# Window attention inside a fused attention and feed-forward kernel: 64-key score blocks on four 64x64 array tiles, one denominator matmul per head, values kept twice

## The chip, the cores and the metric

The kernel runs on one core of one Trainium2 chip. The metric is the device time of one execution in microseconds. The kernel before takes 311.0 us (median of 3 runs, 309.78 to 311.76). A profiled execution gives a span, which is some 1.7 us shorter than the device time that goes with it.

Engines: PE multiplies matrices, PEld loads its weights, VectorE (DVE), ScalarE (ACT) and GpSimd (POOL) work on elements, and SP issues DMA transfers, in the traces in the order of its program (in the changed kernel's second step from the query load at 77.71 us to the second value copy at 93.01).

## The reference

```python
# q, k, v: (8 batches, 8 heads, 576 positions, 64); float32
scores = (q @ k.T) / sqrt(64)
scores = where(abs(pos_q - pos_k) <= 32, scores, -1e9)
attn = softmax(scores) @ v                       # per head
x = attn.transpose(0, 2, 1, 3).reshape(4608, 512)
out = gelu_tanh(x @ w_in) @ w_out                # 512 -> 2048 -> 512
```

A query sees only keys within 32 positions. So only a band of each 576x576 score matrix is computed, in blocks of keys with the queries that can see them.

## The kernel before

Everything is built around PE. A step handles one tile of 512 rows of the feed-forward part, and into its output matmuls (112 of 256 columns; the first step has 64 of 512) a plan inserts the attention of the next batch: `s` is a group of scores, `m` its mask multiply, `v` the weighing of values, `x` the normalised result. A group is a pair of heads; group -1 is the tail of the batch before.

The scores use 128-key blocks, one matmul per head and block, both heads side by side on the two 64-row halves of the array (the cuts of code are shortened, `...` stands for what is left out):

```python
MAIN = [[(0, 0, 0, 40), (128, 1, 24, 72)], [(256, 2, 56, 104), (384, 3, 88, 120)]]
...
PLAN = {6: "s0 v-1", 24: "s1", 26: "m0", 31: "x-1", 40: "m1", 42: "v0 s2", 48: "x0", 56: "m2",
        61: "v1 s3", 64: "x1", 80: "m3", 81: "v2 s4", 88: "x2", 97: "v3", 104: "m4", 112: "x3"}
```

Neighbouring blocks overlap in queries (0 to 40 and 24 to 72, in units of four query rows). So the values and the row sums of a query are accumulated over two blocks, each with one pair of matmuls for the values `o` and one for the sums `d` (weights: a matrix of ones):

```python
for w, bk in ((0, o), (1, d)):
    for h in range(2):
        nc.tensor.matmul(bk[...], V[:, c, head, :] if w == 0 else ones, pes[hf][:, h, ...],
                         start=(i == 0), stop=(i == len(todo) - 1))
```

The fourth group is "fused" in the kernel before: values and ones of a head stand side by side as one 128-column weight, so that one matmul per head and block makes both `o` and `d`.

The first two batches get their values through float32 staging tiles and casts on GpSimd. From batch 2 on they are loaded and cast by DMA (`load_v`, issued by GpSimd), and queries and keys come by seven loads on SP (`load_qk`).

The softmax here doesn't subtract the row's maximum and nothing guards it: scores larger than these inputs give would overflow.

## Time and profile before

| what | before |
|---|---|
| time, median | 311.0 us |
| profiled span | 308.3 us |
| first output matmul of the first step | 39.04 us |
| first step (from there to the next first output matmul) | 34.26 us |
| second step | 32.22 us |
| third to seventh step | 31.60, 31.59, 31.75, 31.60, 31.59 us |
| granted PE clock, mean | 0.996 to 1.000 in ten runs |

The rows of steps are read from the timeline of PE, as the start of the first output matmul of each step. They cut the span into a prologue, two special steps and a steady part. The prediction below shows and reads the lines of the profile themselves.

### The profile page before, as it was taken

The numbers are of one execution on the slowest core, as the hardware profiler recorded it, in microseconds if no ns is written. First come the engines' busy times: TensorE is split into PE (matmuls) and PEld (weight loads), VectorE is DVE, ScalarE is ACT, GpSimd is POOL, SyncE is SP. The second block draws the span as 40 slices with busy tenths as digits, with TensorE's granted clock in tenths as the row PEclk, the third lists the DMA queues.
The fourth block names the chain that finished last, engine by engine and source line by source line (L and its number), as shares of the span: only waits on it lengthen the run. The fifth ranks groups of instructions, "written<-read, shape, count | busy, mean of one in ns | idle before, by whom it ended". The sixth has DMA issues, their size and how long they took to land.

```text
span 308.3 us, 6660 instructions
## 1 busy us (share of the span) xinstructions
PE 297.5 (97%) x2587; PEld 187.8 (61%) x2587; DVE 202.9 (66%) x462; ACT 202.4 (66%) x323; POOL 112.3 (36%) x174
## 2 busy tenths in 40 slices
PE   7889999999999999999999999999999999999993
PEld 2553545546784588458854885478647864784583
DVE  5663686886869676957785778766876655542451
ACT  1776477578677777778677868677767776606600
POOL 4558455069127421832084207620700070015000
PEclk9999999999999999999999999999999999999999
DMA  7999999999996999699969984999471031004013
GB/s 211 254 357 368 375 338 213 290 164 167 222 161 156 148 198 180 157 142 216 169 155 153 240 141 117 164 226 178 115 161 19 2 90 48 0 19 120 0 40 101
DMA packets 120254, 50.65 MB, mean 164 GB/s; under 512 B 101519, under 2 KB 113551, under 8 KB 120222
## 3 DMA queue, kind: packets, MB, share of 16 engines
q1 hardware_dynamic: 84329, 37.50, 54.9%
q0 software_dynamic: 34960, 11.54, 32.4%
q10 hardware_dynamic: 933, 1.18, 1.1%
q8 instruction: 20, 0.33, 0.5%
q14 instruction: 12, 0.10, 0.1%
HBM read 37.62 MB, written 9.44 MB: 153 GB/s over the span
## 4 chain that ended last, share of the span: by engine, by line
PE 84%; SPq 4%; DMA 3%; DVE 3%; ACT 2%; POOL 1%; issue 1%; POOLq 0%
PE mm L574 31%; PE mm L479 21%; PE ph L479 16%; PE ps_s L365 4%; PE mm L545 4%; DMA wst<-in_moe_w_in_dram 3%; PE ps_o L411 3%; PE ps_d L411 2%; SPq L136 1%; SPq L145 1%; POOL w_in L197 1%; PE ps_o L402 1%; SPq L188 1%; DVE t L509 1%; PE ps_d L402 1%
## 5 line engine op out<-in xcount | busy, mean ns | idle before, releaser
L479 PEld LDWEIGHTS <-w_in 128*128 128x128 f16 x576 | 56.0, 98 | 67.3 <-issue 1.8
L535 POOL DMA_DIRECT2D out_dram<-y x77 | 44.7, 588 | 114.1 <-DVE y L603 107.1
L479 PE MATMUL mm<-xT,w_in 128*128 128x512 f16 x320 | 78.0, 379 | 0.6 <-DVE xT L441 0.6
L487 ACT ACTIVATE gT<-mm 128x512 f16<-128x512 f32 x80 | 47.6, 599 | 36.2 <-PE mm L479 35.6
L479 PE MATMUL ph<-xT,w_in 128*128 128x512 f16 x256 | 64.4, 379 | 0.9 <-ACT gT L487 0.7
L574 PEld LDWEIGHTS <-s 128*128 128x128 f16 x512 | 48.9, 98 | 7.0
L519 DVE TENSOR_TENSOR s<-gT 128x512 f16<-128x512 f16 x64 | 26.8, 419 | 35.0 <-ACT gT L487 35.0
L371 ACT ACTIVATE pe<-ps_s 128x704 f16<-128x704 f32 x64 | 43.3, 728 | 9.0 <-PE ps_s L365 8.2
L574 PE MATMUL mm<-t,s 128*128 128x256 f16 x376 | 45.8, 273 | 0.0
L487 ACT ACTIVATE gT<-ph 128x512 f16<-128x512 f32 x64 | 36.3, 602 | 12.3 <-PE ph L479 12.1
L574 PEld LDWEIGHTS <-gT 128*128 128x128 f16 x384 | 36.0, 98 | 7.3
L176 POOL DMA_DIRECT2D V<-in_v_dram x30 | 28.5, 972 | 20.2 <-PE ps_d L411 14.3
L429 ACT ACTIVATE lt<-ps_d 128x480 f32<-128x480 f32 (+3 forms) x33 | 18.2, 553 | 22.6 <-PE ps_d L411 22.5
L574 PE MATMUL mm<-w_out,gT 128*128 128x256 f16 x256 | 32.8, 273 | 0.0
L380 DVE TENSOR_TENSOR pe<-pe,mask 128x704 f16<-128x704 f16 x64 | 30.7, 517 | 1.4 <-ACT pe L371 1.4
L441 DVE TENSOR_TENSOR xT<-ps_o,lt 128x480 f16<-128x480 f32 (+10 forms) x38 | 20.3, 547 | 16.1 <-ACT lt L430 16.0
L430 ACT ACTIVATE lt<-lt 128x480 f32<-128x480 f32 (+3 forms) x40 | 23.5, 587 | 1.3
L91 ACT ACT_TABLE_LOAD x17 | 21.8, 1283 | 1.1 <-PEq L814 0.8
L411 PEld LDWEIGHTS <-V 128*64 128x64 f16 x280 | 15.0, 109 | 9.0 <-issue 3.9
L365 PE MATMUL ps_s<-QT,KT 64*128 64x192 f16 (+5 forms) x336 | 17.9, 227 | 0.9 <-DVE KT L301 0.9
L411 PE MATMUL ps_d<-pe,ones 128*64 128x160 f16 (+2 forms) x208 | 17.6, 234 | 0.0
L411 PE MATMUL ps_o<-pe,V 128*64 128x192 f16 (+3 forms) x188 | 16.8, 241 | 0.7 <-DVE xT L441 0.4
(89 smaller groups left out, 325.5 us busy)
## 6 DMA issues: line engine op xcount, KB each, us to landing
kr<-in_k_dram SPq DMA_DIRECT2D x32, 256.0 KB, 7.9
qr<-in_q_dram SPq DMA_DIRECT2D x6, 1024.0 KB, 7.4
V<-in_v_dram POOLq DMA_DIRECT2D x30, 112.0 KB, 6.9
wst<-in_moe_w_in_dram SPq DMA_DIRECT2D x3, 1024.0 KB, 8.2
wst<-in_moe_w_out_dram SPq DMA_DIRECT2D x3, 1024.0 KB
qr<-in_q_dram SPq DMA_DIRECT2D x8, 256.0 KB
vr<-in_v_dram SPq DMA_DIRECT2D x16, 128.0 KB, 7.4
out_dram<-y POOLq DMA_DIRECT2D x24, 48.0 KB, 2.3
```

Source lines behind the costliest of these rows:

```text
L91: nc.scalar.add_instruction(mybir.InstLoadActFuncSet(name=nc.get_next_instruction_name(), act_func_set_id=which, ins=[], outs=[]))
L176: nc.gpsimd.dma_start(V[:, c, 0:7, :], v[b, 0:7, k0:k0 + 128, :].rearrange("h p d -> p h d"))
L365: nc.tensor.matmul(ps[:, h, off:off + 4 * n].rearrange("k (j p) -> k j p", j=4), KTs[b % 2][r0:r0 + 64, pr, k0:k0 + 128], QTs[b][r0:r0 + 6 ...
L371: nc.scalar.activation(pe, ps[:, :, 0:w], AF.Exp, scale=SCALE)
L380: nc.vector.tensor_tensor(pe, pe, m.rearrange("p (o w) -> p o w", o=1).broadcast_to(list(pe.shape)), op=ALU.mult)
L411: nc.tensor.matmul(bk[r0:r0 + 64, at:at + 4 * n].rearrange("d (j p) -> d j p", j=4)[:, :, p0 - q0:p1 - q0], V[:, c, 2 * pr + h + (pr == 3 ...
L430: nc.scalar.activation(lt[:, 0:n], lt[:, 0:n], AF.Exp, scale=-1.0)
L479: nc.tensor.matmul(ph, w_in16[:, dc, fc * 128:fc * 128 + 128], xT[:, dc, t * 512 % RING:t * 512 % RING + 512], start=(dc == 0), stop=(dc = ...
L487: nc.scalar.activation(gTs[t][:, fc, :], phs[fc], AF.Gelu_apprx_tanh)
L519: nc.vector.tensor_tensor(dst, x, y, op=op)
L535: (eng or turn_about[0] if t == NT - 1 else eng or nc.gpsimd).dma_start(out_v[b, j, q0 + p:q0 + p + e, cols], yo[m:m + e, cols])
L574: nc.tensor.matmul(pys["apart"][:, 0:256] if apart else py[:, blk, :], lhsT, wino[w][:, f, :], start=(new and i % (8 if one else 16) == 0) ...
```

## The change

Intent: fewer PE columns for the attention. Scores are made in 64-key blocks, so four 64x64 tiles of the array work at once (two heads times two key blocks). The queries are cut so that each query column is covered by one pair of 64-key blocks, and is written once. Then the row sums take one matmul per head. For the values, a query column needs 128 consecutive keys that start at a multiple of 64; so the values are kept twice, the second time shifted by 64 keys.

```diff
-MAIN = [[(0, 0, 0, 40), (128, 1, 24, 72)], [(256, 2, 56, 104), (384, 3, 88, 120)]]
+FIRST = [((0, 0, 24), (64, 0, 40)), ((128, 24, 56), (192, 40, 72)), ((256, 56, 88), (320, 72, 104))]
+MAIN = FIRST + [((384, 88, 120), (448, 104, 120))]
+SLOTS = [(0, 0, 24), (4, 24, 40), (1, 40, 56), (5, 56, 72), (2, 72, 88), (6, 88, 104), (3, 104, 120)]
...
-PLAN = {6: "s0 v-1", 24: "s1", 26: "m0", 31: "x-1", 40: "m1", 42: "v0 s2", 48: "x0", 56: "m2", ...
+PLAN = {5: "s0 v-1", 25: "m0 x-1", 27: "s1 v0", 40: "m1 x0", 49: "s2 v1", 62: "m2 x1", ...
...
+    def pair_v(b, copy, hs=slice(0, H)):
+        V = Vs[b % 2]
+        copy(V[64:128, 4:8, hs, :], V[64:128, 0:4, hs, :])
+        copy(V[0:64, 4:7, hs, :], V[0:64, 1:4, hs, :])
...
+    for i, q0 in ((2, 0), (3, 128), (0, 0), (1, 120)):      # masks: 21 small copies, the two halves in turn
+        for step in kinds[i]:
+            for half, piece in enumerate(step): ...
...
+        for h in range(2):                                  # row sums: one matmul per head
+            nc.tensor.matmul(d[64 * h:64 * h + 64, ...], ones, pe[:, h, :], start=True, stop=True)
...
         if t and b + 1 < B:
             load_qk(b + 1)
+        if t == 1:
+            pair_v(unpaired.pop(), nc.sync.dma_start)       # batch 2: two DMAs on SP
```

Batch 0 is paired by VectorE in the prologue, batch 1 by GpSimd in the first step, batch 2 and all later ones by two DMAs on SP, for batch 2 behind the seven loads that SP issues in the second step, and for later ones at the end of a step's program.

## The prediction

> **What bounds the kernel now.** I read the page first, then the chain of waits, then the timeline of each engine over one batch, with the start times of single matmuls.
>
> ```profile
> PE 297.5 (97%) x2587; PEld 187.8 (61%) x2587; DVE 202.9 (66%) x462; ACT 202.4 (66%) x323; POOL 112.3 (36%) x174
> PE   7889999999999999999999999999999999999993
> PE 84%; SPq 4%; DMA 3%; DVE 3%; ACT 2%; POOL 1%; issue 1%; POOLq 0%
> ```
>
> Engines, slices, chain: after the prologue TensorE (PE) has no gap, and it carries 84% of the chain. The rest of the chain is prologue (a 10.4 us wait for first-layer weights up to 25.8 us). So from 45 us on, a nanosecond of PE saved is a nanosecond of time, and any new PE wait is added in full.
>
> A batch step repeats every 31.6 us (124.12 to 155.71 in the chain). In it, 64 matmuls of 512 columns start 0.2155 us apart (13.8 us) and 112 of 256 columns 0.109 us apart (12.2 us). The other 5.55 us are attention: scores s, and weighing v (values "o" and row sums "d") for four head pairs and the tail.
>
> ```profile
> 142.08 1.25 PE L574 MATMUL mm<-w_out,gT 128*128 128x256 f16 x10
> 143.26 0.26 PE L411 MATMUL ps_o<-pe,V 128*64 128x160 f16 x2
> 143.35 0.24 PE L411 MATMUL ps_d<-pe,ones 128*64 128x160 f16 x2
> 143.42 0.25 PE L411 MATMUL ps_o<-pe,V 128*64 128x192 f16 x2
> 143.51 0.25 PE L411 MATMUL ps_d<-pe,ones 128*64 128x192 f16 x2
> ...
> 143.81 0.22 PE L411 MATMUL ps_d<-pe,ones 128*64 128x128 f16 x2
> 143.96 0.47 PE L365 MATMUL ps_s<-QT,KT 64*128 64x160 f16 x8
> 144.36 0.83 PE L574 MATMUL mm<-w_out,gT 128*128 128x256 f16 x6
> ```
>
> Columns: start, length, engine, line, operation, count. A pair of 192 columns (one head per array half) advances the start by 0.08 us, which is 192 columns at one per 0.42 ns: both heads stream together, 3 to 4 ns apart. At each change of array shape there is a hole: the last output matmul starts at 143.058, should free the array 0.109 later, and the weighing starts at 143.261: 94 ns lost. Likewise 98 ns into the scores, 96 out of them, plus 10 ns on the return to the full array and 23 behind the first short pair. Summed over a step with its 14 shape changes: scores 4 x 290 + 170, weighing 3 x 578 + 579 (the fused group) + 341, changes 1495, together 5.48 us, against 5.55 seen. So attention is column-bound plus shape changes, not bound by weight loads.
>
> [...] 3 to 4 ns between tiles, 94 to 98 ns a change. [...] In this trace, 64- and 32-column pairs of 128x64 weights (43.92 to 44.36 us) come every 32 ns whatever their width, where 64 columns would need 27; 96-column pairs take 42, as columns say. [...] issues go one after another and stretch to 4 us when the DMA engines are full. [...] Here the first eight 512-column matmuls take 3.59 us, 0.43 each, against 0.215 later.
>
> **The change, part by part, on PE (one batch step).**
> - Scores: per head 672 columns in two row tiles become 960 in four tiles, 480 columns of time. With full overlap 480 x 0.417 = 200 ns and some ns per step, 208 in place of 290: 4 x 82 = 0.33 us. The tail stays 170.
> - Denominators: one 480-column pair (205 ns). Values: one 96-column pair (42) and six 64-column pairs at the weight-load pace of 32 (192). Sum 439 in place of 578 (three groups) and 579 (fused): 3 x 139 + 140 = 0.56 us. The tail gains 0.01.
> - Shape changes: the fused group had none. Now five episodes go full, score, weigh, full at 96 + 94 + 107 = 297: 1485 in place of 1495. Nothing.
> - Sum: 0.9 us a step, 5.4 us over the six steps with the full plan. The first step (33 to 60 us) gains about 0.8 the same way and gives some back: its values are now paired by eight GpSimd copies (estimated 0.5 us each from the 0.61 us casts of 128x512) between a cast that ends at 46.2 and its use at 46.55. I count a net gain of 0.4.
> - ACT and DVE: one exponential of 960 columns for two (704 and 640; the second starts 638 ns after the first, the next 584 after that, so 853 by slope for 1222) and one mask multiply: slack, not time. Prologue: some 20 small mask copies and eight pairing copies more on DVE (about 1 us and 3.5 us), but weights arrive only at 25.8 while attention ends near 23.2: nothing.
>
> **First new wait.** The plan moves v0 from output matmul 42 to 27, and the tail's spread x-1 just ahead. Both use the one bank for "o".
>
> ```profile
> 137.93 1.28 ACT L91 ACT_TABLE_LOAD   x1
> 139.23 1.35 ACT L371 ACTIVATE pe<-ps_s 128x704 f16<-128x704 f32 x2
> 140.47 0.50 ACT L429 ACTIVATE lt<-ps_d 128x384 f32<-128x384 f32 x1
> 140.99 0.52 ACT L430 ACTIVATE lt<-lt 128x384 f32<-128x384 f32 x1
> ```
>
> Counted from the first output matmul (137.12): table load until 2.11, exponential 0.85, logarithm 0.53, inverse 0.52, spread 0.56: the bank is free at 4.6. PE gets to v0's "o" at 27 x 0.109 + 0.83 (s0, v-1) + 0.40 (s1 and changes) + 0.21 (d) = 4.4. A wait of about 0.25 us in each of five steps: 1.25 us back.
>
> **Second new wait, the large one.** Values stand twice, shifted by 64 keys; the second copy is made by two DMAs on SP, behind the load. In the built order of SP's instructions, batch 2's two copies stand after all seven loads of batch 3's queries and keys, and the second "o" weight load of batch 2 waits for both. In most steps SP is long done. In the step that starts at 73.3 us it is not:
>
> ```profile
> 74.69 0.40 SPq L166 DMA_DIRECT2D qr<-in_q_dram  x1
> 75.15 11.09 SPq L168 DMA_DIRECT2D kr<-in_k_dram  x4
> 86.29 2.75 SPq L170 DMA_DIRECT2D qt<-in_q_dram  x1
> 89.08 1.77 SPq L171 DMA_DIRECT2D kt<-in_k_dram  x1
> ```
>
> and from the DMA issues (last column: median us to landing):
>
> ```profile
> V<-in_v_dram POOLq DMA_DIRECT2D x30, 112.0 KB, 6.9
> kt<-in_k_dram SPq DMA_DIRECT2D x6, 128.0 KB, 4.2
> ```
>
> Two value loads and these loads share full engines there (DMA share over 1.5 in this stretch), so SP frees at 90.85. A tenth fewer value rows, and the 0.4 us gained, make that about 90. Two issues of 0.6 and 4.2 us to landing: about 94.5. PE wants the shifted values at 73.3 - 0.4 + 4.4 = 77.3. It stands for 17.2 us. Nothing hides it, since everything later is PE work. [...]
>
> Sum: 311.0 - 5.4 - 0.4 + 1.25 + 17.2 + 1.5 = 325.1.
>
> **Rivals.**
> 1. Pure PE gain, no new wait: 311.0 - 5.8 = 305.2. For it: PE is the bound and every saved column counts. Against it: SP's order, and a data dependence that no slack covers. It needs SP to issue its seven loads in a few us; the trace shows 16.
> 2. The copies land earlier, because SP's issues stretch less with less value traffic: at 86 the wait is 9 us and the total about 316. [...] Against: the q and k traffic, the larger part, is untouched.
> 3. The four score tiles don't overlap, or small weight loads bind: scores then take 400 ns or more, the 0.9 turns negative, and without the DMA wait the total would be 311 to 316. For: 64x64 weights appear nowhere in this trace. Against: pairs overlap in both directions. It only adds to my number: 330.
> 4. The extra copies overload the DMA engines in every step: 0.45 MB a batch in 3 and 4 KB runs against about 5 MB; in later steps SP is idle from 150.5 to 158.8, where they fit. Nothing.
>
> **Range and chances.** The order on SP and the dependence are facts of the program; only the landing time is estimated, from 88 to 97, which gives 318 to 328. To stay within 2% it must land before about 88 (a wait under 10); to be faster, SP would have to behave quite differently. Faster 0.06, within 2% 0.07, slower 0.87. Predicted 325.0 us, range 316 to 329.
>
> **What would show it.** Right: one hole in PE's slices near 77 to 95 us, ended by the DMA V<-V; steps of about 30.9 us elsewhere; score groups of some 0.21 us with four starts 4 ns apart; a spread ending PE waits of a quarter us in other steps. Wrong: no such hole, V<-V issued before 85, or steps that stay at 31.6 or grow.

The sum came to 325.1 us. Its last term, 1.5 us for a restart at half clock, is the author's estimate. The trace before gives about the same: eight 512-column matmuls, started 0.427 us apart in place of 0.2155, lose 1.7 us. The 1 and 3.5 us of VectorE's copies in the prologue are estimates too.

## The result, and the profile after

The changed kernel takes 330.06 us (median of 4 runs, 329.70 to 332.46), beside 311.02 us for the kernel before on the same chip (now 4 runs, 309.78 to 311.76). The ratio is 1.063 (95% interval 1.0585 to 1.0674), so it is slower. Ratios are the mean time of one kernel's fast runs over that of the other's of the same rounds, so not quite the ratio of the medians quoted. Executions over 1.5% slower than the fastest of the same kernel are left out of the means.

The page of the changed kernel, its first row, two of its rows of 40 slices, and the chain by engine:

```profile
PE 295.6 (90%) x2883; PEld 183.5 (56%) x2883; DVE 195.0 (59%) x436; ACT 185.9 (57%) x283; POOL 106.6 (32%) x167
PE   5968996999109999999999999999999999999994
PEclk9999999999858999999999999999999999999999
PE 82%; DVE 5%; SPq 5%; ACT 2%; issue 2%; DMA 2%; POOL 0%; POOLq 0%
```

PE has almost the same busy time as before (295.6 and 297.5 us) in a span 20 us longer, and the slices show where: a hole of about two slices (8.2 us each) near 82 to 98 us, and thinner work in the first, the third and the seventh slice (prologue and first step). The clock falls inside and behind the hole (0.50 from 88 to 101.7 us). VectorE's share of the chain has grown from 3 to 5%.

The steps, beside those before:

| part | before | after | difference | predicted difference |
|---|---|---|---|---|
| prologue, to first output matmul | 39.04 | 42.23 | +3.19 | 0 |
| first step | 34.26 | 36.06 | +1.80 | -0.4 |
| second step | 32.22 | 48.61 | +16.39 | +17.8 |
| third to seventh step together | 158.13 | 156.58 | -1.55 | -3.25 |
| rest of the span | 44.65 | 44.73 | +0.08 | 0 |
| sum | 308.30 | 328.21 | +19.91 | +14.15 |

The predicted column is the text's own terms, put where it puts them (the second step: -0.9 + 17.2 + 1.5).

**The large hole.** SP's timeline in the second step; columns are start, length, queue, line, operation:

```profile
77.71 0.40 SPq L163 DMA_DIRECT2D qr<-in_q_dram  x1
78.17 12.32 SPq L165 DMA_DIRECT2D kr<-in_k_dram  x4
...
92.43 0.53 SPq L180 DMA_DIRECT2D V<-V  x1
93.01 0.59 SPq L181 DMA_DIRECT2D V<-V  x1
```

and PE's timeline there, in brackets the time for which it stood still and what ended it:

```profile
84.14 0.23 PE L386 MATMUL ps_o<-pe,V 128*64 128x96 f16 x2 [0.17 <-DVE xT L415]
98.93 0.53 PE L386 MATMUL ps_o<-pe,V 128*64 128x64 f16 x12 [14.56 <-DMA V<-V]
```

The first pair of values needs only the unshifted slot 0 and goes at 84.14. The next needs the shifted slot 4. SP takes 12.3 us to issue four key loads, at a DMA share of 2.03 in that stretch (of the four, the first takes 0.58 us and the longest 5.70), reaches the two copies only at 92.43, and they land at 97.95 and 98.80. This is the wait that was foreseen.

**The prologue.** VectorE, before (its mask copies start at 1.96 us and the first query cast at 4.46), against VectorE in the changed kernel:

```profile
2.04 4.55 DVE L243 COPY mask<-full 64x96 f16<-64x96 f16 x21 [0.84 <-POOL full L232]
...
6.79 0.43 DVE L256 CAST q<-qr 128x512 f16<-128x512 f32 x1
```

The cast on which everything hangs is 2.33 us later. The 21 copies mostly start 0.20 us apart; the ten copies before started mostly 0.10 to 0.13 apart. PE stands 2.43 us for that cast, and runs at half clock for longer:

```profile
10.43 0.69 PE L357 MATMUL ps_s<-QT,KT 64*64 64x96 f16 x18
...
14.06 0.42 PE L357 MATMUL ps_s<-QT,KT 64*64 64x96 f16 x18 [0.17 <-DVE KT L293]
```

The same 18 matmuls take 0.69 us and then 0.42. The record of the clock has its first change, to full speed, at 12.98 us here and at 7.01 in the kernel before; PEclk and the mean clocks in this document count the time ahead of it as full speed, but matmuls of 512 columns there start 0.43 us apart, and 0.22 after it. Further on, PE in the changed kernel waits for pairing copies:

```profile
23.19 0.40 PE L386 MATMUL mm<-pe,V 128*64 128x64 f16 x14 [0.77 <-DVE V L181]
23.52 0.61 PE L447 MATMUL mm<-xT,w_in 128*128 128x512 f16 x2
...
25.64 0.40 PE L386 MATMUL ps_o<-pe,V 128*64 128x64 f16 x14 [1.14 <-DVE V L181]
```

Batch 0's attention ends at 26.0 us. Before, it ended at 21.2, and by the time the weights came (25.8) PE had already done 18 of the first-layer matmuls:

```profile
19.63 0.60 PE L479 MATMUL mm<-xT,w_in 128*128 128x512 f16 x2
...
21.79 0.59 PE L479 MATMUL mm<-xT,w_in 128*128 128x512 f16 x2 [0.58 <-DVE xT L441]
22.22 1.02 PE L479 MATMUL ph<-xT,w_in 128*128 128x512 f16 x4
23.08 0.59 PE L479 MATMUL mm<-xT,w_in 128*128 128x512 f16 x2
23.51 1.21 PE L479 MATMUL ph<-xT,w_in 128*128 128x512 f16 x4
24.89 1.04 PE L479 MATMUL ph<-xT,w_in 128*128 128x512 f16 x4 [0.17 <-POOL w_in L197]
```

Now it had done two.

**The first step.** VectorE's mask multiply takes 0.66 us when alone. The next one, during which GpSimd goes through copies and casts without a pause, takes 2.63:

```profile
44.91 0.66 DVE L371 TENSOR_TENSOR pe<-pe,mask 128x960 f16<-128x960 f16 x1 [1.41 <-ACT pe L365]
...
47.60 2.63 DVE L371 TENSOR_TENSOR pe<-pe,mask 128x960 f16<-128x960 f16 x1 [0.59 <-ACT pe L365]
```

GpSimd, the same microseconds:

```profile
46.79 0.69 POOL L180 COPY V<-V 64x512 f16<-64x512 f16 x1
47.54 0.50 POOL L181 COPY V<-V 64x384 f16<-64x384 f16 x1
47.99 1.17 POOL L199 CAST w_out<-wst 128x512 f16<-128x512 f32 x2
49.11 0.61 POOL L266 CAST V<-vr 128x512 f16<-128x512 f32 x1
49.78 0.92 POOL L180 COPY V<-V 64x512 f16<-64x512 f16 x1
```

Two copies and, between them, three casts stand under the multiply. In the kernel before, where GpSimd casts but copies no values, a mask multiply of some 0.5 us took 0.96 at most beside a cast.

**A steady step.** The first head pair's weighing in the fourth step (row sums, then values):

```profile
162.47 0.39 PE L380 MATMUL ps_d<-pe,ones 128*64 128x480 f16 x2
162.96 0.50 PE L386 MATMUL ps_o<-pe,V 128*64 128x96 f16 x14
```

The sums take 0.2 us of PE, but the values start 0.49 later: the bank for them was freed by the spread of the tail only at 162.8.

### The profile page after: what moved, and what is told of

Read it like the earlier page. It is cut to its first block, busy times and chain, and to the rows that moved or that the text cites. A ratio compares the mean times of both kernels' runs of the same rounds, so it can differ in the third digit from the quotient of the medians.

```text
span 328.2 us, 7176 instructions
## 1 busy us (share of the span) xinstructions
PE 295.6 (90%) x2883; PEld 183.5 (56%) x2883; DVE 195.0 (59%) x436; ACT 185.9 (57%) x283; POOL 106.6 (32%) x167
## 4 chain that ended last, share of the span: by engine, by line
PE 82%; DVE 5%; SPq 5%; ACT 2%; issue 2%; DMA 2%; POOL 0%; POOLq 0%
PE mm L542 30%; PE mm L447 20%; PE ph L447 16%; PE ps_s L357 4%; SPq L165 4%; PE mm L513 3%; PE ps_o L386 3%; PE ps_d L380 3%; DMA V<-V 2%; DVE mask L243 1%; DVE KT L293 1%; ACT pe L365 1%; PE pt L287 1%; PE spin L224 1%; PE pt L285 1%
## 5 line engine op out<-in xcount | busy, mean ns | idle before, releaser
L503 POOL DMA_DIRECT2D out_dram<-y x77 | 46.6, 613 | 134.8 <-DVE y L571 134.2
L365 ACT ACTIVATE pe<-ps_s 128x960 f16<-128x960 f32 (+1 forms) x32 | 31.3, 977 | 56.1 <-PE ps_s L357 51.5
L542 PE MATMUL mm<-t,s 128*128 128x256 f16 x376 | 47.3, 275 | 0.0
L455 ACT ACTIVATE gT<-ph 128x512 f16<-128x512 f32 x64 | 36.3, 602 | 12.3 <-PE ph L447 12.1
L386 PE MATMUL ps_o<-pe,V 128*64 128x64 f16 (+2 forms) x424 | 13.4, 200 | 18.2 <-DMA V<-V 14.6
L371 DVE TENSOR_TENSOR pe<-pe,mask 128x960 f16<-128x960 f16 (+1 forms) x32 | 23.5, 735 | 7.9 <-ACT pe L365 7.9
L399 ACT ACTIVATE lt<-ps_d 128x480 f32<-128x480 f32 (+3 forms) x40 | 22.0, 550 | 4.5 <-PE ps_o L386 3.5
L409 DVE TENSOR_TENSOR xT<-ps_o,lt 128x480 f16<-128x480 f32 (+5 forms) x38 | 20.2, 549 | 5.2 <-ACT lt L400 4.5
L173 POOL DMA_DIRECT2D V<-in_v_dram x24 | 21.5, 927 | 1.4 <-PE mm L447 1.4
L555 DVE TENSOR_TENSOR y<-mm,y 128x512 f32<-128x512 f32 x8 | 5.5, 692 | 24.7 <-PE mm L542 24.7
L357 PE MATMUL ps_s<-QT,KT 64*64 64x128 f16 (+3 forms) x648 | 16.1, 218 | 1.6 <-DVE KT L293 1.6
```

The costliest lines, as they stand in the source:

```text
L357: nc.tensor.matmul(ps[64 * half:64 * half + 64, h, 4 * n * r:4 * n * r + 4 * n].rearrange("k (j p) -> k j p", j=4)[:, :, p0 - q0:p1 - q0], ...
L365: nc.scalar.activation(pe, ps[:, :, 0:w], AF.Exp, scale=SCALE)
L371: nc.vector.tensor_tensor(pe, pe, m.rearrange("k (o j) p -> k o (j p)", o=1).broadcast_to(list(pe.shape)), op=ALU.mult)
L386: nc.tensor.matmul(o[64 * h:64 * h + 64, cols].rearrange("d (j p) -> d j p", j=4)[:, :, p0 - q0:p1 - q0], Vs[b % 2][:, slot, 2 * pr + h, : ...
L399: nc.scalar.activation(lt[:, 0:n], d[:, 0:n], AF.Ln)
L455: nc.scalar.activation(gTs[t][:, fc, :], phs[fc], AF.Gelu_apprx_tanh)
```

## The experiments

Twelve kernels, all on one chip, where the kernel before takes 310.6 to 310.8 us (its runs were 310.20 to 313.06). The changed kernel itself was timed on another chip, at 311.02 for the kernel before. The fast times of one kernel scatter by 1.5 to 4.7 us in runs 1 to 7 and by 0.6 to 2.2 in runs 8 to 12, those of the kernel before mostly by 1; a likely reason is given below.

### 1. The copies first on SP

```diff
+        if t == 1:
+            pair_v(unpaired.pop(), nc.sync.dma_start)
         if t and b + 1 < B:
             load_qk(b + 1)
-        if t == 1:
-            pair_v(unpaired.pop(), nc.sync.dma_start)
```

> The changed kernel with one edit: in the second step SP issues batch 2's two value copies before batch 3's seven query and key loads, not after them. My theory (the copies are late because they stand last on SP's queue, and PE's 14.6 us wait is nothing but that): SP has to stand for the value load, which landed at 80.5 us, then issues both copies in about 1.5 us, and they land some 4.5 us later, near 86. PE wants them at about 84. The wait of PE at the shifted values falls from 14.6 us to 1 to 3 us, and the time from 330.1 to about 317.5 us (315.5 to 319.5). Rival A (two copies of 0.45 MB between full DMA engines take long wherever they stand, or the value load itself is late): the wait stays above 8 us and the time above 323. Rival B (the time was lost to the new attention on PE, and the wait only shows it): the hole closes, but the steps after it grow, and the time stays above 325.

323.0 us (321.66 to 323.86), ratio to before 1.037. SP and PE of this run:

```profile
82.83 0.55 SPq L180 DMA_DIRECT2D V<-V  x1
83.44 0.58 SPq L181 DMA_DIRECT2D V<-V  x1
```

```profile
91.86 0.53 PE L386 MATMUL ps_o<-pe,V 128*64 128x64 f16 x12 [4.96 <-DMA V<-V]
```

The second step falls from 48.61 to 39.98 us. The place in the queue is the cause of most of the wait, but my landing time was a miss: the copies take some 7.5 us, not 4.5. Batch 3's value load and the 1 MB query load issued right behind are in flight with them, which is the likely reason, but no run takes these away. Rival B falls (later steps stay at 31.3), and rival A holds for the 5.0 us that are left. The time is also above the estimate because the prologue took 43.93 us here.

### 2. The copies in the middle of SP's loads

```diff
         for c in range(4):
             nc.sync.dma_start(kr[:, c, :, :], ...)
+            if pair and c == 1:
+                pair_v(unpaired.pop(), nc.sync.dma_start)
```

> A half dose of the same: the two copies stand on SP behind the query load and two of the four key loads of batch 3. SP's four key loads were issued over 12.3 us from 78.2 us on, so two of them take about 6 us: the copies go out near 84.5 and land near 90. My theory (the length of the wait is SP's place in the queue): PE waits some 5 to 8 us, and the time is about 322 us (320 to 325), between the changed kernel and the one with the copies first. Rival (landing is set by the DMA engines' load, not by the place on SP): the wait is the same as in the run with the copies first, or as in the changed kernel.

The profiled run was slow, as were two of the four runs; the fast ones took 326.22 and 328.73 us (ratio 1.053), over the 320 to 325 expected. Its prologue is long (first output matmul at 46.58 us, at half clock from 26.0 to 32.8). The second step, read from the trace, is 44.88 us, with a wait of

```profile
100.99 0.54 PE L388 MATMUL ps_o<-pe,V 128*64 128x64 f16 x12 [10.71 <-DMA V<-V]
```

The dose works: waits of 5.0, 10.7 and 14.6 us for copies first, in the middle and last (the middle one from an execution of the slow state, so its size is less sure than the order). The wait was longer than the 5 to 8 I gave, because the first copy's own issue stretched to 3.7 us.

### 3. Mask copies half by half

```diff
-        for step in kinds[i]:
-            for half, piece in enumerate(step):
+        for half in range(2):
+            for step in kinds[i]:
```

> The changed kernel with the 21 small mask copies of the prologue in another order: first all pieces of the lower 64 partitions of a mask, then all of the upper 64. In the changed kernel copies that alternate between the halves start 0.20 us apart, and the one pair in the same half 0.083 us apart, as the copies of the kernel before did (0.10 to 0.12). If a change of half is what keeps VectorE from overlapping one copy with the next, the spacing falls to about 0.1 us for all but some seven, the masks end about 1.5 us earlier, the first query cast starts near 5.2 us in place of 6.8, the first output matmul near 40.7 in place of 42.2, and the time falls by about 1.5 us to 328.5. Rival A (0.20 us is the cost of a 64-partition copy): the spacing stays at 0.20 and nothing moves. Rival B (pairing copies or weights bind the prologue anyway): the cast starts earlier, but the first output matmul stays at 42.2.

331.88 us (329.58 to 333.14), ratio 1.066. VectorE:

```profile
2.04 3.40 DVE L243 COPY mask<-full 64x96 f16<-64x96 f16 x21 [0.84 <-POOL full L232]
5.50 0.11 DVE L244 MEMSET ones<- 128x64 f16 x1
5.64 0.43 DVE L256 CAST q<-qr 128x512 f16<-128x512 f32 x1
```

Copies within a half now start 0.10 us apart, those at a change of half 0.17 to 0.22, with one exception of each kind (0.20 and 0.62). So the spacing is the change of half; rival A falls. What in VectorE sets it is not shown. The cast moves 1.15 us forward, but the first output matmul comes at 43.39 (rival B's sign). So the gain was lost between 6 and 43 us; the clock was at half from 7.8 to 11.2 and from 24.9 to 28.3 us, and runs 6 and 9 look into that.

### 4. The other masks late

```diff
-    for i, q0 in ((2, 0), (3, 128), (0, 0), (1, 120)):
+    make_masks((2, 0))
 ...                                     # behind the first batch's attention
+    make_masks((3, 128), (0, 0), (1, 120))
     cast_open(1)
```

> The changed kernel with only the mask that batch 0's groups use built at the start (9 copies); the three others (12 copies) are built after the first batch's attention, ahead of batch 1's casts. If the prologue's 3.2 us is mostly the mask copies ahead of the first query cast: the cast starts near 4.3 us in place of 6.8, the first output matmul near 40 us in place of 42.2, and the time falls by about 2.3 us to some 327.8. Rival (the eight pairing copies on VectorE bind): the cast starts at 4.3, but the first output matmul moves by under 1 us, and PE's waits for V pairings (0.77 and 1.14 us) grow by what was gained.

334.5 us over four runs, one of them slow (337.26); the fast ones took 332.08 to 336.76 (ratio 1.073). The cast starts at 3.95 and the last values of batch 0 come at 23.05 in place of 25.64, so the attention is 2.6 us earlier, yet the first output matmul comes at 42.72. The stretches of this run (PE busy, loads, other engines, then the granted clock, DMA share and GB/s):

```profile
24.00:28.00 4.00, 4.00 (x14) 1.50 (x12) 1.47 (x3) 0.86 (x1) 3.51 (x6) 0.66 1.05 378
28.00:32.00 4.00, 4.00 (x20) 1.83 (x19) 2.40 (x5) 3.11 (x7) 2.28 (x4) 1.00 1.09 347
```

PE is "busy" all the time, but at a clock of 0.66: 14 matmuls in 4 us. The rest went to the late masks themselves, which kept a key cast waiting (PE stood 1.27 us for it at 35.0). Both my theory and its rival are wrong on where the 2.3 us go.

### 5. Batch 2 paired by VectorE

```diff
-        if t == 1:
-            pair_v(unpaired.pop(), nc.sync.dma_start)
 ...
                 elif kind == "m":
                     mask(*group(g))
+                    if t == 1 and g == 0:
+                        pair_v(unpaired.pop(0), nc.vector.tensor_copy)
```

> The changed kernel with batch 2's two value copies (and no other's) made by VectorE, right behind the first mask multiply of the second step, in place of two DMAs on SP. With the copies first on SP the wait at the shifted values was still 5.0 us, because they were issued at 82.8 us, when the value load had landed, and took some 7.5 us among batch 3's loads. VectorE needs no DMA engine: from its 0.28 to 0.35 us for a 64x512 copy I estimate 1.2 and 0.9 us for the two, done some 2 us after the value load. My theory: the wait of 14.6 us goes to under 1 us, the second step falls from 48.6 us to about 32.8 (31.3 as the later steps, and some 1.5 of waits for VectorE), and the time from 330.1 to about 314 us (312 to 316). Rival (value load itself too late for the new plan): PE waits for VectorE's copy by 2 us or more, time over 316.

319.42 us (318.42 to 319.95), ratio 1.026. VectorE:

```profile
87.41 0.65 DVE L371 TENSOR_TENSOR pe<-pe,mask 128x960 f16<-128x960 f16 x1
88.09 0.69 DVE L180 COPY V<-V 64x2048 f16<-64x2048 f16 x1
88.79 0.55 DVE L181 COPY V<-V 64x1536 f16<-64x1536 f16 x1
89.27 0.54 DVE L415 TENSOR_TENSOR xT<-ps_o,lt 128x384 f16<-128x384 f32 x1
```

Two copies of 1.24 us in all replace DMAs that took 5 to 8, and no DMA wait is left. The second step is 34.45 us, 14.2 under the changed kernel's. PE now waits 0.95 and 1.45 us for VectorE, whose queue is mask, copies, spread. This settles the cause of the large wait: same data, same load, another engine and place. The total is 5 us above my estimate because prologue and first step were slower in this run (44.75 and 38.08 us, at half clock from 24.0 to 30.8 us and from 51.3 to 54.7), and the second step is 1.6 us over the 32.8 expected.

### 6. The prologue's VectorE relieved

```diff
+    make_masks((2, 0))                                  # by half; the rest behind spread(0, 3)
 ...
+    def pair_split(b, hs):
+        nc.scalar.copy(V[64:128, 4:8, hs, :], V[64:128, 0:4, hs, :])
+        nc.vector.tensor_copy(V[0:64, 4:7, hs, :], V[0:64, 1:4, hs, :])
 ...                                                     # used by paired(g), which moves ahead of the mask multiply
```

> The changed kernel with three edits ahead of the first output matmul: only batch 0's mask at the start, its pieces by half; the other three masks behind the first batch's attention; and of each pairing of batch 0 one copy on ScalarE and one on VectorE, ahead of the mask multiply. The two runs on masks alone moved the attention (its last values matmul from 25.6 us to 25.0 and 23.1) but not the first output matmul, with the granted clock at 0.6 to 0.7 between 24 and 28 us, behind a stretch where PE waited for pairings. If the cost of the prologue is the holes of PE and the half clock that follows, this run has neither: last values of batch 0 near 22 us, clock 1.0 from 8 to 40 us, first output matmul near 40 us in place of 42.2 to 43.9, and a time of about 327.5 us. Rival (prologue is bound by loads in any case, and the clock falls by chance): first output matmul at 42 or later.

329.41 us (328.29 to 331.26), ratio 1.058. The last values come at 23.16 and the first output matmul at 42.87: a miss. The holes are not gone, they have new owners (1.44 us for ScalarE's inverse of the third group, which stands behind a pairing copy; 1.3 for ScalarE's copy), and the clock is at half from 22.4 to 29.2 us. That the half clock follows holes fits every run so far, but chance is not ruled out by this one; run 9 is made for that.

### 7. Batch 1's pairing off GpSimd

```diff
-                        pair_v(1, nc.gpsimd.tensor_copy, slice(0, 2))
+                        pair_split(1, slice(0, 2))           # ScalarE and VectorE
 ...                                                          # the same for the other three
```

> The changed kernel with batch 1's eight pairing copies taken off GpSimd: one of each pairing on ScalarE, one on VectorE, spread over the first step. If GpSimd's copies between two places in SBUF are what stretched VectorE's mask multiply from 0.66 to 2.63 us, that multiply is back near 0.7 us, PE's waits of 1.2, 0.8 and 0.7 us in this step go, and the step from the first output matmul of batch 0 to that of the next falls from 36.1 us to about 34.3, as before (34.3) or a little under; the time falls by about 1.8 us to 328.3. Rival (the multiply was late because VectorE's queue is fuller, whoever copies): it stays over 1.5 us or PE waits for ScalarE instead, and the step stays at 36.

331.81 us (329.06 to 332.19), ratio 1.065; the time says nothing, within the scatter. The trace does. The multiply that took 2.63 us:

```profile
47.91 0.66 DVE L376 TENSOR_TENSOR pe<-pe,mask 128x960 f16<-128x960 f16 x1 [0.22 <-ACT pe L370]
```

and the first step is 34.21 us in place of 36.06, as before the change (34.26). VectorE has four more copies in this run and is still faster, so its load was not the cause. The multiply took 2.63 us beside the row of GpSimd's copies and casts, and takes 0.66 here, where two casts start at 48.20 us, the first of them under the multiply, and take 1.66 us together for the 1.16 of two others. By what the one engine holds the other is not shown. Run 7 takes away the copies, and with them the unbroken row; it doesn't tell which of the two held the multiply.

### 8. All of it, and the first weighing later

Runs 5, 6 and 7 together, and

```diff
-PLAN = {5: "s0 v-1", 25: "m0 x-1", 27: "s1 v0", 40: "m1 x0", 49: "s2 v1", 62: "m2 x1",
+PLAN = {5: "s0 v-1", 25: "m0 x-1", 31: "s1 v0", 42: "m1 x0", 51: "s2 v1", 63: "m2 x1",
```

> All three edits of the other runs of this call together (batch 2's copies on VectorE, the prologue, batch 1's copies split), and one more: the first head pair's scores and weighing four output matmuls later (31 in place of 27), and the second's two later, so that the bank for values is free when it gets there. In the steady steps the wait at the first values was some 0.37 us of the 31.3 us. My theory: steps of about 30.95 us, second step about 32.5, first output matmul near 40, and 330.1 - 16.0 - 2.2 - 1.8 - 1.8 = 308.3 us (306 to 311), so 1% under the kernel before. Rival (the wait only moves to the next group): steps stay at 31.3 and the time at 310 or more.

311.2 us (311.17 to 312.11), ratio 1.0009: equal to the kernel before. Steady steps are 30.94 us in place of 31.30. The first weighing in the fourth step now reads

```profile
146.03 0.39 PE L388 MATMUL ps_d<-pe,ones 128*64 128x480 f16 x2
146.25 0.40 PE L394 MATMUL ps_o<-pe,V 128*64 128x96 f16 x14
```

Values follow sums after 0.22 us, not 0.49, and 0.36 us a step is back. The first step is 34.22, the second 33.80 (32.5 expected). The prologue again is the miss: first output matmul at 42.36.

### 9. The same with idle matmuls

```diff
+    spin(3, 512, score=True)
     weighed(2)
 ...
+    spin(5, 512, score=True)
     weighed(3)
```

> The run with all edits together, and eight idle matmuls of 512 columns more on PE (three ahead of the third weighing of batch 0, five ahead of the fourth), where PE stood still for 0.6 and 1.3 us. The work they do is thrown away. In the run without them PE was idle for 3.1 of the 8 us from 16 to 24 us, the clock fell to 0.50 at 21.9 us and stayed there until 28.3, and the first output matmul came at 42.4. My theory (holes of PE in the prologue bring the half clock, and that, not the length of the work, is what the prologue lost): the clock stays at 1.0 from 15 to 30 us, the first output matmul comes at 40 to 40.8, and the time falls from 311.2 to about 309.5 us (308.7 to 310.5). Rival (the clock falls by chance, or the weights bind): the clock falls all the same, or the first output matmul stays at 42, and the time is 311 or more.

310.47 us (310.18 to 310.80), ratio 0.998. The stretches of the run without the idle matmuls (run 8):

```profile
20.00:22.00 2.00, 1.05 (x20) 0.43 (x17) 1.28 (x3) 1.28 (x3) 0.89 (x2) 0.94 1.04 390
22.00:24.00 2.00, 1.33 (x19) 1.09 (x20) 0.69 (x1) 1.87 (x4) 0.97 (x2) 0.50 1.05 391
...
26.00:28.00 2.00, 2.00 (x7) 0.65 (x5) 1.99 (x8) 0.00 (x0) 1.58 (x4) 0.50 1.07 381
```

and with them:

```profile
20.00:22.00 2.00, 2.00 (x26) 1.03 (x25) 1.13 (x3) 1.48 (x3) 1.09 (x2) 1.00 1.05 393
22.00:24.00 2.00, 1.29 (x23) 0.77 (x22) 0.75 (x2) 1.92 (x5) 0.77 (x2) 1.00 1.05 395
...
26.00:28.00 2.00, 2.00 (x11) 0.97 (x10) 1.99 (x7) 0.59 (x2) 1.58 (x3) 1.00 1.03 368
```

PE busy is the second number, the clock the third from the end. With work that is thrown away the clock stays at 1.0; 11 real matmuls fit into 26 to 28 us in place of 7, and the first output matmul comes at 40.00 in place of 42.36. All four runs have a mean clock of 0.997 or 0.998, where the run without has 0.987 to 0.994. So the theory holds for these two holes. The time gained only 0.7 us, not 2.4, since the first step became 35.55 us long: what comes earlier out of the prologue then waits for VectorE's casts and spreads of that step.

### 10 and 11. VectorE's order, without and with idle matmuls

Batch 2's pairing behind the tail's spread and ahead of a 1.22 us weight subtraction, the first pairing of batch 0 all on VectorE, the fourth behind the third's logarithm, and the late masks in other gaps.

> The run with all edits together, with VectorE's and ScalarE's work reordered and no idle matmuls added: in the second step one of the weight subtractions of 1.22 us stands behind batch 2's pairing, and the pairing behind the tail's spread, so that PE's waits of 0.5 and 1.45 us there should shrink to some 0.5 in all (second step 32.6 us in place of 33.8); in the prologue the first pairing is all VectorE's, the fourth stands behind the third's logarithm, and the late mask copies stand in earlier gaps. Prologue: some 0.7 us fewer holes. If holes alone bring the half clock, it may or may not fall here: first output matmul between 40 and 42. Time 308.0 to 310.5 us. Rival (something else binds the second step): it stays at 33.5 or more.

> The reordered kernel of the same call plus the eight idle matmuls: clock 1.0 through the prologue, first output matmul at 39.5 to 40.5, second step about 32.6, later ones 30.94: 307.5 us (306.5 to 309), about 1% under the kernel before. Rival (loads bind the prologue from 25 us on, as they did in the kernel before, where the first output matmul came at 39.0): nothing earlier than 39, and if the second step stays at 33.8 the time is 309 or more, equal to the kernel before.

310.04 us (309.78 to 310.44), ratio 0.997, and 310.24 us (309.08 to 311.31), ratio 0.997. The second step fell to 32.93 in both, as wanted (I said 32.6). The first step is 35.46 and 35.44. With idle matmuls, in the profiled run a hole ahead of them (1.12 us of waiting up to 14.9) was followed by half clock from 15.2 to 18.6 us, and later PE stood 1.49 us for a query cast on GpSimd, up to 34.1; the first output matmul came at 42.09, against 41.22 without. These eight idle matmuls were not where this order needed them. Holes alone don't settle it: in run 9 PE stood 1.16 us up to 11.3 and the clock stayed at 1.0, and of run 11's six executions three have a mean clock of 0.993 or 0.994 and three of 0.997 to 1.000. The expectation of 307.5 us was missed.

### 12. The best of these

Run 9, with batch 1's pairing behind the spreads, and a plan of its own for the second step, in which the first weighing waits until output matmul 44.

> The run with all edits and idle matmuls, and two changes of order: in the first step each pairing of batch 1 stands behind the spread it does not depend on; in the second step the subtraction of 1.22 us stands behind batch 2's pairing, the pairing behind the tail's spread, and the first values of batch 2 wait until output matmul 44 in place of 31, when all of that should be done. In the run before, the first step was 35.55 us (PE waited 1.6 us in all for VectorE, 0.4 to 0.6 at a time) and the second 33.81 (waits of 0.5 and 1.45). My theory (both are VectorE's order, not its load): first step about 34.8, second 31.2 to 32, later ones 30.94, and the time falls from 310.5 to about 307.6 us (306.8 to 308.8), 1% under the kernel before. Rival (VectorE is full in these two steps, so the wait moves elsewhere): first step 35.5, second 33 or more, time 309.5 or more.

309.09 us over six runs (308.33 to 309.74), ratio 0.994 (95% interval 0.990 to 0.997). It beats both kernels, the one before by 0.6%, which by the 2% used here still counts as the same. Mean clock 0.994 to 1.000, first output matmul at 39.70, second step 32.43, later ones 30.94. The time lies over my range (306.8 to 308.8), and the second step over the 31.2 to 32. The first step stayed at 35.37: there the rival was right.

## Why the prediction was right or wrong

The direction was right: slower, by a new wait for the second copy of the values. The number was not: 330.1 us lies 1 us above the range, 5 above the value. In the order of the prediction's own steps:

- **"Second new wait, the large one": right in cause, slightly too large.** The wait was 14.6 us, not 17.2: the copies landed at 98.8, 4.3 us later than the 94.5 of the text (its own terms, 90 + 0.6 + 4.2, give 94.8), but PE came to them at 84.4, 7.1 us later than its 77.3. Most of both is that the step began 5.4 us late. Counted from the step's start, the copies landed 20.5 us in, for 21.6, and PE came 6.1 us in, for 4.4, having stood 1.1 us for VectorE. "Two issues of 0.6 and 4.2 us to landing" was too short (5.5 and 5.8 us to landing); "SP frees at ... about 90", 17.1 us into the step, was too long (13.9). Runs 1, 2 and 5 show the cause: moving the copies in SP's queue changes the wait from 14.6 to 10.7 to 5.0 us, taking them off DMA ends it. The half clock behind it is real: recorded at 0.50 from 88 to 101.7 us. The step's excess over a steady one is 17.31 us; without the waits of 14.56, 0.95 and 0.17 it leaves 1.6, against the 1.5 taken.
- **"Prologue: ... nothing": wrong, +3.2 us.** This is the step that failed first. It compared two end times, attention at 23.2 and weights at 25.8, and counted all between as slack. It was not slack: before the change PE used that time for 18 first-layer matmuls, and after it for two; the other 16, at 0.2155 us each, are an estimated 3.4 us. And the cost was mis-sized: the mask copies put the first cast back by 2.33 us where the text had 1, because copies that change the partition half start 0.20 us apart, those within a half 0.10 (run 3), and pairing copies stand in the path of PE.

  On top of that comes the clock. In the changed kernel PE was at half clock up to 13.0 us, not 7.0. In all six profiled kernels whose first cast starts at 5.6 us or later, the array is still or again at half clock up to a point between 10.3 and 15.7 us; in the eight where it starts at 4.5 or earlier, it is at full speed from 7.0 us at the latest (run 11 falls again later). That is a pattern over kernels, not an experiment of its own. Later holes bring the half clock in some executions and not in others; run 8 against run 9 shows this for two holes near 20 us. No single run gives back the 3.2 us: runs 3, 4 and 6 start the cast earlier and lose the gain to half clock near 25 us and to new waits; with masks and pairings moved and the clock kept (runs 9 and 12) the first output matmul comes at 40.00 and 39.70. The clock is also the likely cause of the scatter: the changed kernel's other runs have mean clocks of 0.969 to 0.974 against 0.977 in the profiled one, and in runs 3, 4, 6 and 7 the half clock behind the large hole lasts up to 106.8 us and the second step 0.8 to 1.8 us longer. The other runs of the changed kernel have no trace, so for them this is argued, not shown.
- **"The first step ... a net gain of 0.4": wrong, +1.8 us.** The durations of the GpSimd copies were about right (0.50 to 0.92 us against an estimated 0.5). What was missed is what they do to another engine: a mask multiply beside GpSimd's row of copies and casts takes 2.63 us for 0.66 (run 7 takes the copies away, and with them 1.85 us). The estimate looked at the copies' own chain only.
- **"Sum: 0.9 us a step": half right.** Four tiles do run together (they start 3 to 4 ns apart), the pairs of 64 columns come every 32 ns, and a change of shape costs 92 to 94 ns, as said. A steady step still gained only 0.30 us, where 0.9 less 0.25 was expected. Two terms were mis-sized. "First new wait", put at 0.25, was worth 0.36: PE stands 0.26, and the values behind it take 0.11 longer than in the next group (436 ns for 329); run 8 takes both away and the steps go from 31.30 to 30.94. And the gain without it is then 0.66, not 0.9: a score group takes 334 ns with its exit, not 306 (208 and a 98 ns change), four times, and the last weighing of a step takes 626 ns where the middle ones take 556.
- **Rivals.** Rival 1, the pure gain, would have been 305.2. The best run, without the large wait and the wait for the bank, is at 309.1: the gain is 0.66 us a step, and prologue and first step keep 0.7 and 1.1 us of their loss. Rival 2, copies that land earlier, did not come to pass in absolute time (98.8 us); counted from the step's start, SP was free 3.2 us earlier than the text had it, and the longer landing took back two thirds of that. Rivals 3 and 4 did not come to pass: no step from the third on grew.

The parts add up: 3.2 + 2.2 + 1.7 - 1.4 = 5.7 us of error on the span, of which 19.9 - 14.15 = 5.75 are to be explained.

What stays open: in the best version the first step is 1.1 us longer than before the change, and no run tells VectorE's order there apart from its load. Nor does a run tell GpSimd's copies from its casts in what held VectorE, or test the late start of full clock alone.

## What to carry to other kernels

Before calling work in a prologue free because a later load bounds it, look at what PE did in the gap between the two; the gap may be used, and holes there may cost twice, through the clock (from 26 to 28 us run 8 did 7 matmuls at a clock of 0.50, run 9, with idle matmuls in its holes, 11 at 1.00). When a change adds copies, price three things, not one: their own time, the queue that they stand in, and the engine that they slow (a mask multiply of 2.63 us for 0.66) or whose order they disturb. A copy inside SBUF that stands behind long loads in a DMA queue may be cheaper on a compute engine with room at that moment: here 1.24 us of VectorE ended a 14.6 us wait for two DMAs.

## What the traces measured of the hardware

- A change of tile shape: 92 to 98 ns lost at most changes (94 from the output matmuls into the scores), with some 15 changes in a step of 31 us.
- Short matmuls: pairs of 128x64 tiles with 64 columns come every 32 ns (so do their weight loads), where 64 columns at the 0.42 ns of longer pairs would need 27, and the kernel before's pairs of 32 columns come no faster.
- The clock: no wait of PE in run 8 between 16 and 22.4 us was over 1.30 us, yet with PE idle for 1.04 and 0.95 us of two successive stretches of 2 us the clock fell to 0.50 at 21.75 us and stayed there for 6.8 us. With eight idle matmuls it stayed at 1.00 (first output matmul at 40.00 in place of 42.36 us).
- DMA issue: SP's issue of four 256 KB loads took 12.3 us at a DMA share of 2.03, and what stood behind them on SP was issued after it (the value copies at 92.43 us; in run 1, ahead of those loads, at 82.83).
